# Attention feeding a two-layer network on one core: another planner, another order for the first pairs, a later load of the output weights

## The chip, the cores and the metric

The kernel runs on one core of one Trainium2 chip. The metric is the device time of one execution in microseconds (us), as the median of eleven runs of the kernel before. The profile is of one further look at the same program: its span runs from the first to the last instruction on the core.

## The reference

There are 8 batches of 8 heads with 576 positions and head width 64. Each head is computed twice: once with queries, keys and values averaged over groups of 4 positions (144 positions), and once in a window of fewer than 4 positions to either side. The two are added, the heads are laid side by side, and the 4608 x 512 matrix `x` goes through two matrix products with the function h/(1+exp(-h)) between them.

```python
out_d = sm_attn(mean4(q), mean4(k), mean4(v))          # 144 positions
out_up = np.repeat(out_d, 4, axis=2)
mask = np.abs(pos[:, None] - pos[None, :]) < 4
out_local = softmax(where(mask, scale * q @ k.T, -1e9)) @ v
x = (out_up + out_local).transpose(0, 2, 1, 3).reshape(4608, 512)
h = x @ w_in                                           # 512 x 2048
g = h * (1.0 / (1.0 + np.exp(-h)))
return g @ w_out                                       # 2048 x 512
```

## The kernel before

**Pairs.** Two heads make a pair `p`, 32 in all; four pairs make a batch. The work of one pair on TensorE (PE) is cut into units, each a function of the builder: `T` (36 transposes of queries and keys, 72 instructions with their weight loads, line 572), `S` (scores: 20 local matmuls, then 8 with the averaged queries and keys), `Z` (the sums of both softmaxes), `VP` (averages of the values), `PV` (the products with the values) and `RB` (spreads the reciprocal sums over the rows). From pair 10 on, unit `V(n)` joins S of pair n, T of n+1, Z of n-1 and PV of n-2, and from pair 10 the reciprocals take a way through DRAM instead of RB.

**What stands around a unit.** A pair's `q` and `k` (two DMAs of 288 KB, into 4 buffers `qk`) and its `v` (four of 80 KB, into `vs`) come on SyncE's queue, SP. `c` casts q and k on GpSimd, POOL (line 544; on VectorE, DVE, for pairs 0 and 1); `cw` casts the values (line 554). `eq` and `ek` bring T's result back on ScalarE, ACT; `mk` averages the keys on DVE (line 586) and `mq` the queries (two POOL instructions, lines 597 and 599, for pairs 0 to 7; DVE line 590 after). S waits for all of these; its last 8 matmuls for mq. `x` and `xd` are the exponentials on ACT (lines 624 and 626), `k` the mask on DVE (line 628). After Z: the reciprocal `r`, then `rh`, `rx`, `rm`, `rl` (lines 707 to 714) split it into three parts for RB, `eb` copies RB's result (ACT, line 735), `m` multiplies (DVE, line 745) and `a` adds both attentions into `xT` (POOL, line 769). RB and S share the PSUM tensor AB. PV and Z of pairs 0, 2 and from 4 on use CD, those of pairs 1 and 3 use HP, which the first matrix product uses too.

**The network.** `g1_j_f` is one tile of the first product: 512 rows (j, 9 of them) by 128 columns (f, 16), four matmuls; ACT takes a tanh (`t`, line 783) and DVE multiplies (`s`, line 785). `g2` is a quarter of a tile of the second product, four matmuls; four quarters make 128 rows of the output. g1 of j=0 needs `a` of pairs 0 to 3; g1 of j=1 also that of pairs 4 to 7. The weights are loaded from POOL's queue in eight pieces, `w0` to `w3` for w_in and `w4` to `w7` for w_out.

**Order.** Nothing is ordered at run time: each engine runs a fixed list. The builder makes the units in a written order (lines 900 to 935). Then `Plan.order` (line 218) plays them through: each engine picks among the next few units (14 on PE, 30 on POOL, 40 elsewhere; on PE in the order made) one that is ready in its own accounting. Costs (`cost`, `dcost`), the latencies `LAT` and due times of the weights (`ready`, line 882) only decide the order; they are not waited for on the chip. A unit that is placed early on an engine holds up all that is listed behind it, as engines run in order.

Of the kernel before, what the change touches and what calls it, by code (L numbers as in the profile page):

```python
# [18 lines left out]
NVP = 14  # L19
NDIR = 10  # L20
NEQ = 12
NTH = 99
NMQ = 8


# [141 lines left out]
class Plan:  # L167


    LAT = {"PE": 0.25, "ACT": 0.2, "DVE": 0.2, "POOL": 0.2, "SP": 0.1}  # L170

    def __init__(self):
        self.units = []
# [13 lines left out]
    def op(self, u, fn, r=(), w=(), dma=None):  # L187
# [27 lines left out]
        pre.discard(u)  # L215
        u.pre |= pre

    def order(self, look, first):

        todo = {e: first.get(e, "").split() for e in Prog.ENGS}  # L220
        free = {e: 0.0 for e in Prog.ENGS}
        ring = {e: 0.0 for e in Prog.ENGS}
        for u in self.units:
            u.pre = {v for v in u.pre}
            u.npre = len(u.pre)
            for v in u.pre:
                v.succ.append(u)
        pend = {e: [u for u in self.units if u.eng == e] for e in Prog.ENGS}
        head = {e: 0 for e in Prog.ENGS}
        taken = set()  # L230
        res = []
        left = len(self.units)
        while left:
            best = None
            for e in Prog.ENGS:
                lst = pend[e]
                while head[e] < len(lst) and lst[head[e]] in taken:
                    head[e] += 1
                if todo[e]:
                    win = [next(u for u in lst[head[e]:] if u.name == todo[e][0] and u not in taken)]  # L240
                    if win[0].npre:
                        continue
                else:
                    win = [u for u in lst[head[e]:head[e] + look[e]] if u not in taken and not u.npre]
                if not win:
                    continue
                t = max(free[e], min(u.ready for u in win))
                c = min((u for u in win if u.ready <= t + 0.05), key=lambda u: (u.ready - 100000 if u.fifo else u.prio, u.idx))
                t = max(t, c.ready)
                if best is None or t < best[0]:  # L250
                    best = (t, c)
            t, u = best
            del todo[u.eng][:1]
            u.start = t
            free[u.eng] = t + u.cost
            if u.dcost:
                e = u.eng
                begin = max(t + u.cost + 0.4, ring[e])
                other = max(x for y, x in ring.items() if y != e)
                ring[e] = begin + u.dcost + min(u.dcost, max(0.0, other - begin))  # L260
                u.end = ring[e] + (3.2 if e == "ACT" else 1.6)
                if e == "SP":
                    free[e] = max(free[e], ring[e] - 4.0)
            else:
                u.end = t + u.cost + self.LAT[u.eng]
            for v in u.succ:
                v.npre -= 1
                same = v.eng == u.eng and not u.dcost
                v.ready = max(v.ready, t + u.cost + (0.06 if u.eng != "PE" else 0.0) if same else u.end)
            taken.add(u)  # L270
            res.append(u)
            left -= 1
        res.sort(key=lambda u: u.start)
        return res


def bass_hourglass_attn__then__act_silu_kernel(
# [9 lines left out]
    with kctx:  # L287
# [4 lines left out]
        def R(name, psum=False):  # L292
            if name not in res:
                res[name] = Res(name, psum)
            return res[name]
# [57 lines left out]
        def one(eng, name, cost, fn, r=(), w=(), dma=None, prio=None, dcost=0.0):  # L353
            u = L.unit(eng, name, cost, prio, dcost)
            L.op(u, fn, r, w, dma)
            return u
# [103 lines left out]

        def dma(eng, name, out_, in_, w, sem, dcost, r=(), prio=None, cost=0.42):
            return one(eng, name, cost, lambda s: s.dma_start(out_, in_), r, w, sem, prio, dcost)  # L464

        def tick(p, d):
# [53 lines left out]
        def load_w(c):  # L520
            if c < 4:
                return dma("POOL", f"w{c}", w_in_sb[:, :, 512 * c:512 * c + 512],
                           moe_w_in[:, 512 * c:512 * c + 512].rearrange("(kc p) f -> p kc f", p=128),
                           [R(f"w_in{c}")], f"w_in{c}", 3.1, cost=0.9)
            c -= 4
            return dma("POOL", f"w{c + 4}", w_out_bf[:, 4 * c:4 * c + 4, :],
                       moe_w_out[512 * c:512 * c + 512, :].rearrange("(f p) n -> p f n", p=128),
                       [R(f"w_out{c}")], f"w_out{c}", 3.1, cost=0.9)
# [199 lines left out]
        def RB(p):  # L728
            n = p % NR
            u = L.unit("PE", f"RB{p}", 0.45)  # L730
            for m in range(10):
                x, c = divmod(m, 5)
                mm(u, AB[:, x, 72 * c:72 * c + 72], sel[:, m, :], rpart[p % 2][:, 2, :],
                   selr + [rpr[p % 2][2]], [rAB[x]])
            one("ACT", f"eb{p}", 0.77, lambda e: e.activation(  # L735
                Rb[n][:, :].rearrange("p (x n) -> p x n", x=2), AB[:, :, 0:360], AF.Copy),
                r=rAB, w=[R(f"Rb{n}0"), R(f"Rb{n}1")])
# [69 lines left out]
        def T(p):  # L807
            made.add(("T", p))
            u = L.unit("PE", f"T{p}", 0.45 if p > 1 else 0.9)
            pe_T(u, p)  # L810
            after_T(p)

        def VP(p):
            u = L.unit("PE", f"VP{p}", 0.4 if p > 1 else 0.8)
            pe_VP(u, p)
            after_VP(p)

        def S(p):
            u = L.unit("PE", f"S{p}", 0.4 if p > 1 else 0.8)
            pe_S(u, p)  # L820
            after_S(p)

        def Z(p):
            made.add(("Z", p))
            u = L.unit("PE", f"Z{p}", 0.35 if p > 1 else 0.7)
            pe_main(u, None, p)
            after_Z(p)

        def PV(p):
            made.add(("PV", p))  # L830
            u = L.unit("PE", f"PV{p}", 0.45 if p > 1 else 0.9)
            pe_main(u, p, None)
            after_PV(p)
# [22 lines left out]
        def feed():  # L856

            for p in range(NPAIR):
                for name, fn, need in (
                    ("lqk", load_qk, ("c", NQK)), ("c", cast, ("T", NB - 1)),  # L860
                    ("lv", load_v, ("cw", NVS)), ("cw", castw, ("PV", NV)),
                    ("lvq", load_vq, ("cv", NVQ)), ("cv", castv, ("PV", NV)),
                ):
                    src = {"c": "lqk", "cw": "lv", "cv": "lvq"}.get(name)
                    if p < NVP and name in ("lvq", "cv"):
                        made.add((name, p))
                    if (name, p) in made or (src and (src, p) not in made):
                        continue
                    if p >= NTH and name[0] == "l" and ("x", p - (4 if name == "lqk" else 3)) not in made:
                        continue  # L870
                    if p >= need[1] and (need[0], p - need[1]) not in made:
                        continue
                    if name in ("lv", "lvq") and ("lqk", p) not in made:
                        continue
                    made.add((name, p))
                    fn(p)
# [2 lines left out]
        constants()  # L879
        feed()  # L880
        for c in range(8):
            load_w(c).ready = 16.0 + 5.0 * c
        todo = [(j, f) for j in range(NSUP) for f in range(16)]
        todo2 = [(j, tt) for j in range(NSUP) for tt in range(4)]

        def G1(n):
            for _ in range(n):
                if todo:
                    g1(*todo.pop(0))
# [7 lines left out]
            if parts[-1] == 3:  # L897
                todo2.pop(0)

        T(0)  # L900
        feed()
        for n in range(10):
            T(n + 1)
            feed()
            S(n)
            if n > 0:
                Z(n - 1)
            if n > 1:
                PV(n - 2)
                feed()  # L910
            if 0 < n <= NDIR:
                RB(n - 1)
            if 0 < n <= NVP:
                VP(n - 1)
            if n > 4:
                G1((2, 4, 4, 4, 2)[n - 5])
        L.boost = 0
        n = 10
        while todo or todo2:
            if n < NPAIR + 2:  # L920
                V(n)
                if n <= NDIR:
                    RB(n - 1)
                if n <= NVP:
                    VP(n - 1)
                feed()
            m = 4
            G1(1 if m else 0)
            G2((0,))
            G1(1 if m else 0)  # L930
            G2((1,))
            G1(1 if m else 0)
            G2((2, 3))
            G1(m - 3 if m else 0)
            n += 1
        P = Prog()
        for u in L.order({"PE": 14, "ACT": 40, "DVE": 40, "POOL": 30, "SP": 40}, FIRST):
# [36 lines left out]
```

## Time and profile before

| | |
|---|---|
| median of 11 runs | 359.32 us (357.58 to 361.86) |
| the profiled execution's own time | 359.32 us |
| its span, first to last instruction | 357.6 us |
| PE busy | 329.4 us (92%) |
| DVE, ACT, POOL busy | 222.0, 182.1, 156.3 us |
| bytes moved | 60.28 MB, mean 169 GB/s |
| first g1 matmul, first g2 matmul | 43.6 us, 77.9 us |
| V(10) begins on PE | 73.87 us |

1.7 us of the time lie outside the span. In the slices of the profile, each digit is the busy share of an engine in a fortieth of the span (8.9 us); in the table by stage, the busy time of an engine stands beside the number of its instructions in parentheses, then the clock granted to TensorE (1.00 is full), the share of the DMA engines and GB/s. In a list of instructions in order of time, the brackets at the end of a row hold the idle time before it and what ended it.

### The profile page before, as it was taken

The page shows a single profiled execution, that of the slowest core. Times are in us where ns is not written, and L with a number is a line of the kernel's source. Part 1 is how long each engine was busy: PE and PEld are TensorE (multiplying, and loading weights), DVE is VectorE, ACT ScalarE, POOL GpSimd, SP SyncE. Part 2 cuts the span into 40 slices and gives each one's busy share as a digit, 9 for nine tenths or more (in the row PEclk, how much of TensorE's full clock was granted, in tenths as well). Part 3 has the DMA queues.
Part 4 walks back from the last instruction along what each step waited for, and adds up shares of the span by engine and source line. Part 5 has one row for each costly group of instructions (what it writes and reads, how often), then busy time and mean ns, then how long its engine had stood idle before and what let it go on. Part 6 is the DMA issues. An engine that isn't in the chain of part 4 may idle for free.

```text
span 357.6 us, 10993 instructions
## 1 busy us (share of the span) xinstructions
PE 329.4 (92%) x4712; PEld 214.0 (60%) x4742; DVE 222.0 (62%) x392; ACT 182.1 (51%) x326; POOL 156.3 (44%) x203
## 2 busy tenths in 40 slices
PE   1674799989999999999999999999999999999996
PEld 0453677556666666666666666666665566666642
DVE  7585879986766677777767667666655434343400
ACT  2773668766555555455555555555553343434421
POOL 7948775651755566555565666553111100000000
PEclk9996589999999999999999999999999999999999
DMA  8999999997899978878777784132042000110012
GB/s 230 234 262 266 308 272 251 256 230 196 256 231 279 255 224 219 230 200 220 217 226 210 213 209 149 65 119 75 34 129 89 31 29 29 45 44 29 31 59 88
DMA packets 73506, 60.28 MB, mean 169 GB/s; under 512 B 47986, under 2 KB 55794, under 8 KB 73458
## 3 DMA queue, kind: packets, MB, share of 16 engines
q1 hardware_dynamic: 63818, 44.27, 45.4%
q10 hardware_dynamic: 5416, 9.02, 9.1%
q0 software_dynamic: 4224, 6.29, 7.9%
q8 instruction: 37, 0.61, 0.7%
q14 instruction: 11, 0.09, 0.1%
HBM read 51.76 MB, written 9.91 MB: 172 GB/s over the span
## 4 chain that ended last, share of the span: by engine, by line
PE 80%; DMA 6%; DVE 4%; SPq 3%; POOL 2%; issue 2%; ACT 2%; POOLq 0%; ACTq 0%
PE HP L359 36%; PE o L359 28%; PE pe_ L359 8%; PE CD L359 5%; DMA vs<-in_v_dram 4%; SPq L464 3%; PE AB L359 3%; DMA qk<-in_k_dram 3%; PE o L572 2%; DVE gT L785 1%; POOL qkb L544 1%; POOL vt L597 1%; DVE rrest L711 1%; DVE Pt L628 0%; DVE xo L745 0%
## 5 line engine op out<-in xcount | busy, mean ns | idle before, releaser
L359 PE MATMUL HP<-xT,w_in_sb 128*128 128x512 f32 x576 | 162.6, 419 | 0.3 <-DVE gT L785 0.2
L785 DVE SCALAR_TENSOR_TENSOR gT<-th,HP 128x512 bf16<-128x512 f32 x144 | 96.5, 683 | 100.7 <-ACT th L783 99.9
L783 ACT ACTIVATE th<-HP 128x512 f32<-128x512 f32 x144 | 86.1, 598 | 76.6 <-PE HP L359 73.9
L359 PEld LDWEIGHTS HP<-xT,w_in_sb 128*128 128x128 f32 x576 | 106.2, 190 | 27.4 <-DVE gT L785 0.7
L359 PE MATMUL o<-w_out_bf,gT 128*128 128x512 bf16 x437 | 101.8, 379 | 1.9 <-issue 0.2
L359 PEld LDWEIGHTS o<-w_out_bf,gT 128*128 128x128 bf16 x464 | 42.4, 98 | 55.1 <-issue 9.8
L769 POOL TENSOR_TENSOR xT<-xo 128x576 fp32r<-128x576 f32 (+3 forms) x48 | 44.2, 933 | 48.8 <-DVE xo L745 48.8
L800 ACT ACTIVATE osb<-o 128x512 f32<-128x512 f32 x29 | 17.3, 597 | 61.3 <-PE o L359 61.3
L554 POOL CAST vb<-vs 128x640 bf16<-128x640 f32 x30 | 21.7, 724 | 58.7 <-PE CD L359 43.1
L544 POOL CAST qkb<-qk 128x1152 bf16<-128x1152 f32 x30 | 34.4, 1146 | 5.3 <-DMA qk<-in_k_dram 5.0
L572 PE MATMUL o<-idn,qkb 64*64 64x64 bf16 x576 | 17.3, 203 | 15.2 <-POOL qkb L544 8.2
L745 DVE TENSOR_TENSOR xo<-CD,Rb 128x720 f32<-128x720 f32 x30 | 27.0, 899 | 1.3 <-ACT Rb L735 0.7
L559 POOL TENSOR_TENSOR vt<-vq 128x512 f32<-128x512 f32 x18 | 22.9, 1273 | 7.6 <-DMA vq<-in_v_dram 7.6
L359 PE MATMUL pe_<-w_out_bf,gT 128*128 128x512 bf16 x109 | 26.1, 380 | 0.2
L572 PEld LDWEIGHTS o<-idn,qkb 64*64 64x64 bf16 x576 | 13.7, 118 | 17.9 <-POOL qkb L544 8.9
L586 DVE TENSOR_REDUCE kd<-kT 128x144 bf16<-128x576 bf16 x32 | 23.4, 733 | 1.1 <-ACT kT L582 1.1
L582 ACT ACTIVATE kT<-pe_ 128x576 bf16<-128x576 bf16 x32 | 20.9, 652 | 1.8 <-PE pe_ L572 0.4
L624 ACT ACTIVATE Pt<-AB 128x576 bf16<-128x576 f32 x32 | 20.7, 648 | 1.2 <-PE AB L359 1.2
L572 PE MATMUL pe_<-idn,qkb 64*64 64x64 bf16 x576 | 16.5, 203 | 2.0 <-DVE qkb L541 1.0
L359 PEld LDWEIGHTS pe_<-w_out_bf,gT 128*128 128x128 bf16 x112 | 10.0, 98 | 13.6 <-issue 3.2
L590 DVE TENSOR_REDUCE qd<-qT 128x144 bf16<-128x576 bf16 x24 | 17.8, 743 | 0.0
L628 DVE TENSOR_TENSOR Pt<-Pt,mask_bf 128x576 bf16<-128x576 bf16 x32 | 16.3, 511 | 0.9 <-ACT Pt L624 0.9
(79 smaller groups left out, 314.1 us busy)
## 6 DMA issues: line engine op xcount, KB each, us to landing
vs<-in_v_dram SPq DMA_DIRECT2D x126, 80.0 KB, 4.2
qk<-in_q_dram SPq DMA_DIRECT2D x32, 288.0 KB, 4.7
out_dram<-osb SPq DMA_DIRECT2D x36, 256.0 KB, 3.3
qk<-in_k_dram SPq DMA_DIRECT2D x30, 288.0 KB, 5.6
Rb<-scr ACTq DMA_DIRECT2D x44, 180.0 KB, 4.6
vq<-in_v_dram SPq DMA_DIRECT2D x18, 256.0 KB, 5.6
w_in_sb<-in_moe_w_in_dram POOLq DMA_DIRECT2D x4, 1024.0 KB, 9.6
w_out_bf<-in_moe_w_out_dram POOLq DMA_DIRECT2D x4, 512.0 KB, 9.1
```

The lines of the kernel that those rows point to most:

```text
L359: L.op(u, lambda t: t.matmul(out_, lhsT, rhs, start=start, stop=stop, skip_group_check=True), r, w)
L544: one("POOL", f"c{p}", 1.15, lambda g: g.tensor_copy(qkb[j][:, :, :], qk[i][:, :, :]), r=[R(f"qk{i}0"), R(f"qk{i}1")], w=[R(f"qkb{j}0"), R ...
L554: one("POOL", f"cw{p}", 0.72, lambda g: g.tensor_copy(vb[m][:, :, :], vs[i][:, :, :]), r=rr, w=[R(f"vb{m}")])
L559: one("POOL", f"va{p}", 1.3, lambda g: g.tensor_tensor(vt[:, :, :], vq[i][:, :, 0:128], vq[i][:, :, 128:256], ALU.add), r=rr, w=[R("vt")])
L572: L.op(u, lambda e, o=o, w=w, j=j: e.transpose(o, w, idn[half(j), :]), [R("id"), R(f"qkb{n}{x}")], [rE if x else rF])
L582: one("ACT", f"ek{p}", 0.68, lambda e: e.activation(kT[j][:, 3:579].rearrange("p (g r) -> p g r", r=9), pe_[:, 0:288].bitcast(BF16).rearra ...
L586: one("DVE", f"mk{p}", 0.74, lambda e: e.tensor_reduce(kd[j][:, 0:SD], kT[j][:, 3:579].rearrange("p (g r) -> p g r", r=4), AX.X, ALU.add), ...
L624: one("ACT", f"x{p}", 0.66, lambda e: e.activation(Pt[m][:, :, :], AB[:, :, 0:288], AF.Exp, scale=0.125), r=rAB, w=[R(f"P{m}"), R(f"tick{p ...
L745: one("DVE", f"m{p}", 0.92, prio=-450000 if L.boost else None, r=rCD + [R(f"Rb{u}0"), R(f"Rb{u}1")], w=[R(f"xo{x}")], fn=lambda e: e.tenso ...
L769: one("POOL", f"a{p}", 0.15 + n * 0.0019, lambda g, dst=dst, in0=in0, in1=in1: g.tensor_tensor(dst, in0, in1, ALU.add), r=[R(f"xo{x}")], w ...
L783: one("ACT", f"t{j}_{f}", 0.62, lambda e: e.activation(th[tb][:, :], hps[hb], AF.Tanh, scale=0.5), r=[rH[hb]], w=[R(f"th{tb}")], prio=-1)
L785: one("DVE", f"s{j}_{f}", 0.71, lambda e: e.scalar_tensor_tensor(gT[j % 2][:, f, :], th[tb][:, :], 1.0, hps[hb], ALU.add, ALU.mult), r=[rH ...
```

## The change

`Plan.order` is written anew. It used to pick, event by event, with one running time for each DMA ring; it now steps a clock over all engines, lets the rings share one rate (`SHARE`, `WORK`), delays PE at each block of 256 instructions, slows PE's units before its time 52 and keeps certain DVE units and POOL's apart in time (`LOCK`). Its result is again only an order. The written order of the first ten pairs is new, as is the place of g1 and g2 among the later V units. Loads of pairs from 12 on wait for an exponential of a pair 3 or 4 before (`NTH` 99 becomes 12). The due times of w_in go from 16, 21, 26, 31 to 18, 23, 28, 33 and those of w_out from 36, 41, 46, 51 to 55, 60, 65, 70. `pace` is new but off (`CAP` is 0), `hold` stays empty and `WEIGHTS` is not used.

```diff
-NTH = 99
+NTH = 12
+CAP = 0
...
-            load_w(c).ready = 16.0 + 5.0 * c
+            load_w(c).ready = float((18, 23, 28, 33, 55, 60, 65, 70)[c])
...
-        T(0)
-        feed()
-        for n in range(10):
-            T(n + 1)
-            feed()
-            S(n)
-            if n > 0:
-                Z(n - 1)
-            if n > 1:
-                PV(n - 2)
-                feed()
-            if 0 < n <= NDIR:
-                RB(n - 1)
-            if 0 < n <= NVP:
-                VP(n - 1)
-            if n > 4:
-                G1((2, 4, 4, 4, 2)[n - 5])
+        hold = []
+        for x in """
+            T0 T1 S0 T2 S1 Z0 T3 S2 RB0 VP0 PV0 Z1 T4 S3 RB1 VP1 PV1 Z2 S4 RB2 VP2 PV2 Z3 RB3 VP3 PV3 T5
+            G2 S5 Z4 RB4 VP4 PV4 T6 G2 S6 Z5 RB5 VP5 PV5 T7 G3 S7 Z6 RB6 VP6 PV6 T8 G3 S8 Z7 RB7 VP7 PV7
+            T9 G4 S9 Z8 RB8 VP8 T10 G2
+        """.split():
...
-            m = 4
-            G1(1 if m else 0)
             G2((0,))
-            G1(1 if m else 0)
-            G2((1,))
-            G1(1 if m else 0)
-            G2((2, 3))
-            G1(m - 3 if m else 0)
+            G1(2)
+            G2((1, 2, 3))
+            G1(2)
```

In the list, `G2` stands for two tiles of g1, `G3` for three. What the planner makes of it, read from the built programs (the number after the letters is the pair):

```
PE before:   T0 T1 S0 T2 S1 Z0 VP0 T3 Z1 RB0 PV0 VP1 S2 T4 PV1 RB1 Z2 VP2 S3 T5 PV2 Z3 RB2 VP3 S4 T6 PV3 RB3
             Z4 VP4 S5 T7 Z5 RB4 g1_0_0 g1_0_1 PV4 S6 VP5 g1_0_2 RB5 g1_0_3 T8 S7 g1_0_4 Z6 g1_0_5 ...
PE after:    T0 T1 S0 T2 S1 Z0 T3 Z1 VP0 PV0 S2 T4 RB0 VP1 S3 PV1 Z2 RB1 VP2 S4 PV2 RB2 Z3 VP3 PV3 RB3 T5
             Z4 S5 VP4 g1_0_0 g1_0_1 RB4 PV4 T6 g1_0_2 g1_0_3 Z5 VP5 S6 g1_0_4 PV5 T7 RB5 g1_0_5 ...
POOL before: mq1 c3 mq2 cw2 w0 c4 mq3 cw3 c5 a0 w1 cw4 mq4 w2 a1 c6 cw5 mq5 a2 w3 c7 cw6 a3 w4 mq6 c8 cw7
             mq7 a4 w5 c9 cw8 w6 c10 cw9 a5 w7 c11 cw10 a6 ...
POOL after:  mq1 c3 cw2 w0 mq2 cw3 c4 w1 mq3 c5 mq4 a0 w2 cw4 a1 w3 c6 a2 cw5 mq5 a3 c7 cw6 cw7 c8 a4 mq6
             cw8 w4 cw9 mq7 a5 w5 c9 w6 a6 w7 cw10 a7 c10 ...
```

Up to V(10) the order before has 16 tiles of g1, the order after 19. From V(10) on both give each V four tiles of g1 and four quarters of g2.

## The prediction

> **What bounds the kernel now.** First the slices and busy times of the page.
>
> ```profile
> PE 329.4 (92%) x4712; PEld 214.0 (60%) x4742; DVE 222.0 (62%) x392; ACT 182.1 (51%) x326; POOL 156.3 (44%) x203
> ...
> PE   1674799989999999999999999999999999999996
> ...
> PEclk9996589999999999999999999999999999999999
> ```
>
> PE is full from the seventh slice on, and its work does not change. So the time is decided in the first 80 us: whatever PE leaves idle there is added at the end. The table by stage says where.
>
> ```profile
> 20.00:25.00 5.00, 4.66 (x162) 3.66 (x158) 3.76 (x8) 4.11 (x10) 1.70 (x3) 1.00 1.06 325
> 25.00:30.00 5.00, 0.82 (x60) 0.82 (x60) 1.73 (x6) 1.15 (x3) 2.02 (x2) 0.61 0.98 206
> ...
> 60.00:70.00 10.00, 9.48 (x203) 6.44 (x200) 10.00 (x16) 7.53 (x15) 6.67 (x7) 1.00 1.18 244
> 70.00:75.00 5.00, 3.76 (x114) 2.67 (x116) 3.60 (x8) 2.58 (x6) 2.00 (x3) 1.00 1.18 257
> ```
>
> In order PE, PEld, DVE, ACT, POOL, clock, DMA. At 25 to 30 PE stands still; from 60 to 70 DVE is full, and PE's 9.48 is not at its peak. The list of POOL's instructions in order of time names the transfers behind it:
>
> ```profile
> 18.78 1.16 POOL L544 CAST qkb<-qk 128x1152 bf16<-128x1152 f32 x1
> ...
> 22.28 0.72 POOL L554 CAST vb<-vs 128x640 bf16<-128x640 f32 x1 [1.21 <-DMA vs<-in_v_dram]
> 27.98 1.15 POOL L544 CAST qkb<-qk 128x1152 bf16<-128x1152 f32 x1 [4.99 <-DMA qk<-in_k_dram]
> ...
> 45.58 0.68 POOL L597 TENSOR_TENSOR vt<-qT 128x288 f32<-128x288 bf16 x1
> ...
> 49.57 0.72 POOL L554 CAST vb<-vs 128x640 bf16<-128x640 f32 x1 [1.72 <-DMA vs<-in_v_dram]
> ```
>
> By their order these are c4, cw3, c5, mq6 and cw7. The waits of PE (in total, times, longest) agree:
>
> ```profile
> PE o L572 <- POOL qkb L544: 8.2, 4, 4.2
> PE AB L359 <- ACT Rb L735: 1.0, 1, 1.0
> ```
>
> Its longest wait, 24.97 to 29.18, is T5 for c5, and c5 for the keys of pair 5.
>
> **What the Trainium skill says.** "DMA: Bandwidth & Descriptors", section Issuing engines are not separate DMA queues: loads from SP, ACT and POOL run on the same 16 engines and interleave. The trace agrees: pair 4's q and k, issued at 13.5, landed in 3.9 to 4.2 us; pair 5's, issued at 18.2 beside w0, took 7.5 to 9.0. "TensorE: Matmul & The Clock Gate", Part 1: the clock falls to half after an idle window of about 3.4 us and rises after as much work; here it is 0.61 at 25 to 30, and VP takes 0.93 us before the clock has risen, 0.56 after. "SBUF — State Buffer", on the shared port pair: certain VectorE and GpSimd operations exclude each other for a whole instruction; the trace has a 0.28 us `rx` of 2.69 us at 33.33, while POOL is busy without a break. "Runtime: NRT & Kernel Launch", Instruction fetch mechanics: instructions come in blocks of 256, mostly hidden; here PE's idle time put down to issue is 0.6 us in all, so replaying the blocks has little to win.
>
> **The change, part by part.** I follow the new lists with the durations of the old trace. A unit runs when its engine is free and its inputs are there.
>
> *1. c4 behind cw3.* On POOL, c4 ran at 18.78, before the values of pair 3 were needed. Now cw3 stands ahead, and those landed at about 22.3: cw3 to 23.0, c4 (1.15) to 24.1, so T4 at 24.2 instead of 21.39. RB0, formerly at 18.63, is listed behind T4: 24.9. PE idles some 3 us from about 21, where it was busy.
>
> *2. T5 behind PV3.* The 4.21 us wait for c5 leaves PE. Its cover is now the chain of pairs 0 to 3: RB0 24.9, S3 27.2 (AB is free after eb0), PV1 27.9, Z2 28.7 (CD is free after m0), RB1 29.3, VP2 30.1. S4's last matmuls need mq4, which stands behind c5: 28.0 to 29.1, mq4 to 30.2. S4 at 31.1 (eb1), PV2 31.8, RB2 33.1 (AB after x4, xd4: 0.65 and 0.53), Z3 33.9, VP3 34.5, PV3 36.0, RB3 37.4 (r 0.6, rh 0.26, rx, rm, rl some 0.8, with m2's 0.9 between), eb3 to 39.0, m3 to 40.0. T5 38.2, mq5 39.7 to 40.8, a3 to 42.0, S5 40.9, VP4 to 42.5: g1_0_0 at 42.6. Before: PV3 36.28, RB3 37.37, a3 43.62 to 44.82, so the two first tiles, begun at 43.62, ended at 47.0 (the fourth matmul needs a3). After: 42.6 and 3.4 us at half clock, 46.0. That is 1.0 us ahead, with T6, T7, Z5 and RB4 (0.4, 0.4, 0.35, 0.45: 1.6 us at full clock) not yet done. Net 0.6 us lost.
>
> *3. mq6 behind cw7, c8 and a4.* In the old list mq6 came before c8 (45.58) and S6 ran at 47.5. Now POOL does a3, c7, cw6 (to 43.9), then cw7 for the values of pair 7. These landed at 49.5. Do they come sooner? w1 is issued at about 24 instead of 30.24, but w0 landed only at 29.7 on the same queue; the gap in which that queue stood empty, 29.7 to about 30.9, is used, so w3 ends 1 to 2 us sooner than 49.2. Until then pair loads lag as much; after it they catch up. I take 49.4; bounds 47 (all of w_in out of the way early) and 51 (the lag not made up). cw7 to 50.1, c8 51.3, a4 (1.2) 52.5, mq6 (1.1) 53.6. PE comes to S6 thus: RB4 0.5, PV4 0.6, T6 0.4, two g1 at 0.93 (1.84 us for eight matmuls in the chain of waits), Z5 0.4, VP5 0.5: 4.3 us after 46.0, at 50.3. It waits 3.3 us; behind it in the list stand twelve tiles of g1, which need nothing from S6. By 53.6 the kernel before has also done T7, T8, S6, S7, RB5, Z6 and more than one g1: some 4 us of work.
>
> *4. From S6 to V(10).* Here DVE decided before (full from 60 to 70). In the new list from k6 (54.8) to s0_14: eleven s at 0.60, three m at 0.85, mk 0.7 x3, mq 0.7 x2, r 0.55 x3, k 0.4 x3, two triples rx, rm, rl at 0.77: 17.0 us, 0.4 until g1_0_4 has passed, and as much waiting for POOL's port as DVE had from 52 to 73, about 3 (k once 1.49, rl once 1.04, rx thrice over 0.6): 75.2. PE's own work to there is 19.2 from 53.6, so it is covered. g1_1_0 75.3, T10 0.4, RB8 0.45, two g1, V(10) at 78.9. It has three more tiles behind it than the old V(10) at 73.87: 78.9 less 2.8 is 76.1, 2.3 us late. Less of the 4 us than it seems, since in the old stretch PE needed 21.2 us for 17.1 of work; DVE made it slow, and now PE's lag hides there.
>
> *5. w_out later.* w4 follows cw8 on POOL at about 55 (before 44.78), w7 follows a6 at about 66 to 68 (63.18), landing 8.7 us later at 75 to 77. g2_0_0_3 comes at about 83: covered. If a6 slips, w7 slips with it; five us of slip would show. What the later w_out frees, transfers for pairs 8 to 10, held up no PE unit before (T8 50.7, c8 46.7): nothing won.
>
> *6. NTH, the pattern after V(10), pace.* SP now waits for x of pair p-4 before loading pair p; outputs queue behind. Two to three V periods of 8.65 us lie between load and use, against 4 to 10 us for landing: nothing. The same units per V: nothing, at most some tenths either way. pace is off.
>
> Sum: +2.3 us on the span of 357.6. The profiled execution's own time is 359.32, the same as the median, 1.7 above its span: 361.6.
>
> **The rivals.**
> - *DVE forgives more.* The triples and k now fall between POOL's operations: half of the 3 us of port waits go, PE limits at 53.6 + 19.2 = 72.8, V(10) at 76.8, net 74.0: 359.5. For it: nothing but order decides who blocks whom. Against it: POOL's own list is fuller there, with w4 to w7 and c9 moved in.
> - *Faster: the S6 wait does not bind.* mq6 ends 4.2 us after pair 7's values land, and PE comes to S6 at 50.3: it decides if they land by 46.1 (or PE comes 3.3 us later). Then S6 runs at 50.3 and DVE starts 3.3 us sooner: V(10) net at 72.8 to 71, by 1.1 to 3 below 73.87; 356.8 with PE's clock warm throughout. For it: after w3 nothing but pair loads is in flight. Against it: up to then w_in presses harder than before.
> - *Slower still.* The 3.3 us idle cools the clock (0.61 after the 4.2 us of before): up to 1.7 us more; a7, listed behind w7 and cw10, holds g1_1_0 by 1 us: 364.5.
> - *It doesn't do what it says:* g1 is not earlier by more than 1 us. That is part of my forecast, not another time.
>
> **How the numbers follow.** Forecast (361.6, own range 360.0 to 363.2) 0.55; DVE forgives (359.5) 0.14; faster (356.8) 0.20; slower still (364.5) 0.11. A difference below about 0.5%, 1.8 us, cannot be told from none. Of the forecast two thirds lie above 361.1: slower 0.37 + 0.11 = 0.48; same 0.18 + 0.14 = 0.32; faster 0.20. Range 356.5 to 365.0, which leaves out half of the faster case and little above.
>
> **What would show it.** Right: T4 at 23 to 25 with PE idle before it; no wait of T5 for c5; g1_0_0 at 41 to 44; S6 waiting for mq6 until 52 or later with cw7 behind a transfer; V(10) at 78 to 80. Wrong: cw7 before 46, or S6 without a wait; DVE with clear idle time at 60 to 70; g2_0_0 waiting for w_out.

## The result, and the profile after

The changed kernel takes **363.38 us** (median of 13 runs, 360.43 to 365.52), the kernel before 359.33 (50 runs). The ratio is 1.011, with a 95% interval from 1.0085 to 1.0134. So it is slower, by 1.1%. The forecast was 361.6, in a range of 356.5 to 365.0. All ratios in this text are of fast runs; only three runs, all of the experiment e10, were slow.

The profiled execution of the changed kernel has a time of its own of 365.1 us and a span of 363.4. As before, 1.7 us lie outside the span. It is 1.7 us above the median of its runs, so its waits are larger than a middling run has; a comparison with other profiles below says which.

First come the page's busy times and the slices that answer to those shown of before.

```profile
PE 329.5 (91%) x4712; PEld 214.8 (59%) x4742; DVE 227.2 (63%) x392; ACT 182.7 (50%) x326; POOL 158.1 (44%) x203
...
PE   0557757999999999999999999999999999999996
...
PEclk9998598999999999999999999999999999999999
```

PE does the same work: 329.5 us, against 329.4. From the eighth slice on it is as full as it was. The sixth and seventh slices, from 45.4 to 63.6 us, which held a 9 each before, hold a 5 and a 7 now. So the loss again lies in the first 80 us. The table by stage has, in this order, the stretch, its length, the busy time of PE, PEld, DVE, ACT and POOL with the number of instructions, the clock, the share of the DMA engines, and GB/s:

```profile
20.00:25.00 5.00, 2.38 (x99) 1.97 (x100) 2.82 (x7) 1.85 (x5) 3.41 (x6) 1.00 1.08 324
25.00:30.00 5.00, 4.34 (x101) 3.64 (x99) 2.95 (x6) 3.76 (x8) 4.62 (x7) 1.00 1.22 303
...
50.00:55.00 5.00, 1.76 (x36) 1.17 (x36) 3.07 (x5) 1.28 (x3) 4.40 (x6) 0.94 0.72 195
55.00:60.00 5.00, 5.00 (x102) 4.02 (x95) 2.85 (x4) 3.65 (x7) 0.00 (x0) 0.72 1.04 184
60.00:65.00 5.00, 2.45 (x99) 1.80 (x97) 2.14 (x3) 1.99 (x6) 4.07 (x6) 1.00 0.89 189
65.00:70.00 5.00, 4.65 (x69) 3.09 (x65) 4.93 (x9) 3.96 (x8) 1.88 (x3) 1.00 1.00 145
70.00:75.00 5.00, 5.00 (x99) 3.77 (x99) 4.93 (x12) 3.91 (x9) 2.21 (x3) 1.00 1.04 153
```

The stretch from 25 to 30, in which PE stood still before, is full now (4.34 of 5 us). In its place PE idles from 20 to 25 (2.38 us busy, before 4.66), and stands still twice later, from 50 to 55 and from 60 to 65. In between, the clock was 0.72 in the mean. The clock column is to be trusted only from the first change on record, here at 30.51 us: before it, it reads 1.00, but VP takes 0.93 us at 19.04, 0.94 at 29.29 (clock not yet risen) and 0.56 at 48.73, at full clock.

The waits of PE (in total, times, longest) name what it stood for:

```profile
PE AB L453 <- POOL qd L714: 8.1, 4, 3.7
...
PE CD L453 <- issue: 2.2, 2, 1.7
PE o L687 <- POOL qkb L659: 1.8, 2, 1.2
PE AB L453 <- DVE rp L829: 1.8, 3, 1.1
```

The waits for casts of keys, 8.2 us before, are down to 1.8. Waits of S for the averaged queries `qd`, which `mq` writes on POOL, have come in their place: 8.1 us, of which 1.6 belong to S0 at the start. The two longest are these rows of PE's list in order of time (start, length, instruction; in brackets the idle time before it):

```profile
49.23 0.35 PE L453 MATMUL AB<-qT,kT 64*64 64x58 bf16 x20
53.24 0.29 PE L453 MATMUL AB<-qd,kd 64*64 64x144 bf16 x8 [3.67 <-POOL qd L714]
...
59.95 0.35 PE L453 MATMUL AB<-qT,kT 64*64 64x58 bf16 x20
62.84 0.29 PE L453 MATMUL AB<-qd,kd 64*64 64x144 bf16 x7 [2.55 <-POOL qd L714]
```

These are S6 and S7: the 20 local matmuls run, and then the last 8 wait for mq6 and mq7. The two waits, 6.22 us, are all the idle time of PE from 45 to 65; in the kernel before it was 0.57 us there. POOL's list of the same time shows why mq6 and mq7 are late:

```profile
48.99 0.72 POOL L669 CAST vb<-vs 128x640 bf16<-128x640 f32 x1 [2.25 <-DMA vs<-in_v_dram]
49.66 1.15 POOL L659 CAST qkb<-qk 128x1152 bf16<-128x1152 f32 x1
50.76 1.20 POOL L884 TENSOR_TENSOR xT<-xo 128x576 fp32r<-128x576 f32 x1
51.93 0.66 POOL L712 TENSOR_TENSOR vt<-qT 128x288 f32<-128x288 bf16 x1
52.67 0.42 POOL L714 TENSOR_TENSOR qd<-vt 128x144 bf16<-128x144 f32 x1
53.04 0.72 POOL L669 CAST vb<-vs 128x640 bf16<-128x640 f32 x1
53.70 0.78 POOL L579 DMA_DIRECT2D w_out_bf<-in_moe_w_out_dram  x1
60.85 0.71 POOL L669 CAST vb<-vs 128x640 bf16<-128x640 f32 x1 [6.38 <-DMA vs<-in_v_dram]
61.53 0.66 POOL L712 TENSOR_TENSOR vt<-qT 128x288 f32<-128x288 bf16 x1
```

By their order these are cw7, c8, a4, mq6 (two rows), cw8, w4, cw9 and the first half of mq7. Twice POOL stands at a cast of values, cw7 and cw9, whose transfer has not landed. Each time a `mq` that PE needs sooner stands behind it. V(10) starts on PE at 83.59 instead of 73.87. It has three more tiles of g1 behind it, at 0.93 us each; so it is 6.9 us late, and the span is 5.8 us longer. In all nine profiles in which PE has the changed kernel's list (this one, e1 to e6, e9 and e12), the span ends 279.8 us after the start of V(10), within 0.1 us. So what these kernels differ in is decided before V(10).

### The profile page after: what moved, and what is told of

Read it like the earlier page. It is cut to its first block, busy times and chain, and to the rows that moved or that the text cites. A ratio compares the mean times of both kernels' runs of the same rounds, so it can differ in the third digit from the quotient of the medians.

```text
span 363.4 us, 11005 instructions
## 1 busy us (share of the span) xinstructions
PE 329.5 (91%) x4712; PEld 214.8 (59%) x4742; DVE 227.2 (63%) x392; ACT 182.7 (50%) x326; POOL 158.1 (44%) x203
## 4 chain that ended last, share of the span: by engine, by line
PE 79%; SPq 6%; POOL 4%; DMA 4%; DVE 3%; issue 2%; ACT 1%; POOLq 0%; ACTq 0%
PE HP L453 35%; PE o L453 27%; PE pe_ L453 7%; SPq L579 6%; PE CD L453 4%; PE AB L453 3%; POOL xo L476 2%; DMA vs<-in_v_dram 2%; DMA qk<-in_k_dram 2%; PE o L687 2%; DVE rrest L826 1%; DVE gT L900 1%; POOL vt L712 1%; DVE rp L828 0%; PE pe_ L687 0%
## 5 line engine op out<-in xcount | busy, mean ns | idle before, releaser
L453 PE MATMUL HP<-xT,w_in_sb 128*128 128x512 f32 x576 | 160.6, 418 | 0.4
L453 PEld LDWEIGHTS o<-w_out_bf,gT 128*128 128x128 bf16 x464 | 42.6, 98 | 54.9 <-issue 8.4
L884 POOL TENSOR_TENSOR xT<-xo 128x576 fp32r<-128x576 f32 (+3 forms) x48 | 45.1, 952 | 39.7 <-DVE xo L860 39.6
L743 DVE TENSOR_TENSOR Pt<-Pt,mask_bf 128x576 bf16<-128x576 bf16 x32 | 17.8, 557 | 3.7 <-ACT Pt L739 3.7
```

The source lines that it names most:

```text
L453: L.op(u, lambda t: t.matmul(out_, lhsT, rhs, start=start, stop=stop, skip_group_check=True), r, w)
L884: one("POOL", f"a{p}", 0.15 + n * 0.0019, lambda g, dst=dst, in0=in0, in1=in1: g.tensor_tensor(dst, in0, in1, ALU.add), r=[R(f"xo{x}")], w ...
```

## The experiments

All experiments were timed against the kernel before, which was run again beside each group of them (medians from 359.27 to 359.99). The ratios are estimates over the runs and not quite the quotients of the medians: for e3 these would give 360.43/359.80 = 1.0018, inside its interval. In the builder, the table `FIRST` can hold an engine's list of units, which is then taken instead of what the planner chooses. Except for e8 and e11, every kernel below holds all lists of one of the two kernels there, and only the units named in its diff stand elsewhere. So PE, ACT, DVE and SP keep their order. A ratio below 1 is faster than before.

| | edit | median us (runs) | ratio to before, 95% interval |
|---|---|---|---|
| after | | 363.38 (13) | 1.0110 [1.0085, 1.0134] |
| e1 | after, mq6 earlier | 362.16 (19) | 1.0053 [1.0031, 1.0075] |
| e2 | after, mq7 earlier | 362.45 (15) | 1.0066 [1.0042, 1.0091] |
| e3 | after, mq6 and mq7 earlier | 360.43 (14) | 0.9999 [0.9972, 1.0026] |
| e12 | after, w4 later | 362.41 (9) | 1.0085 [1.0049, 1.0121] |
| e6 | after, c4 earlier | 363.40 (6) | 1.0097 [1.0059, 1.0134] |
| e5 | e3, c4 earlier | 359.21 (14) | 0.9980 [0.9961, 1.0000] |
| e9 | e5, w1 to w3 later | 360.89 (22) | 1.0019 [1.0004, 1.0034] |
| e4 | after, no NTH | 363.47 (6) | 1.0089 [1.0056, 1.0122] |
| e7 | before, w_out later | 358.46 (22) | 0.9971 [0.9947, 0.9995] |
| e10 | e7, c6 and c7 earlier | 359.62 (22) | 0.9987 [0.9967, 1.0007] |
| e8 | the change without its planner | 368.10 (6) | 1.0228 [1.0198, 1.0258] |
| e11 | the new planner alone | 363.72 (6) | 1.0113 [1.0065, 1.0161] |

**The waits for mq6 and mq7: e1, e2, e3.** The theory: nearly all of the loss is S6's and S7's waits, made by POOL's order. The rival: they are only where a late head shows, and PE would wait elsewhere without them. e1 moves mq6, e2 mq7, e3 both.

```diff
 e1, POOL: ... c7 cw6
+mq6
 cw7 c8 a4
-mq6
 cw8 w4 cw9 mq7 a5 ...
```

> All five engine lists are those of the changed kernel; on POOL alone mq6 stands before cw7 instead of behind a4. Theory A (POOL's list holds S up, at S6 and again at S7): the 3.67 us wait of S6 goes, but mq7 still stands behind cw9, whose values landed at 60.85, so S7 waits some 5 to 6 us instead of 2.55; the time falls by 0 to 1.5 us, to 362 to 363.4. Rival B (what costs is the DMA share, not the list): S6 waits elsewhere for as long, no change. Rival C (one wait is all): 3.5 us less, about 360.

```diff
 e2, POOL: ... cw7 c8 a4 mq6 cw8
+mq7
 w4 cw9
-mq7
 a5 w5 ...
```

> Lists of the changed kernel; on POOL alone mq7 stands before w4 instead of behind cw9. Theory A: S6's 3.67 us stay, S7's 2.55 go; the time falls by 1.5 to 2.5 us, to 361 to 362. Rival B: no change. With DVE as the bound of that stretch the gain would be under 1 us.

e3 makes both moves.

> Both moves. Theory A: both waits go, 6.2 us of idle PE, of which DVE takes some back; the time falls by 3 to 6 us, to 357.5 to 360.5, at or below the kernel before. Rival B (DMA share): under 1 us. DVE-bound rival: 1 to 2 us.

Measured: against before, the changed kernel's 1.1% falls to 0.53% with mq6 moved, to 0.66% with mq7 moved, and to nothing with both (0.9999). The parts of 0.57 and 0.44 points make up 1.01 of the 1.11 of e3. The interval of e2 just touches that of the changed kernel; those of e1 and e3 lie clear of it. So moving two units of 1.1 us each in POOL's list, with all other lists as they were, takes away the loss. The moves do shift one more thing: w4, now listed behind mq7, goes out at 58.66 in e2 and 58.40 in e3 instead of 53.70. The waits of PE in e2:

```profile
PE AB L453 <- POOL qd L714: 4.9, 2, 3.6
```

S6 waits as before, 3.6 us; S7's wait is gone. In e1 S6 does not wait. Nor does S7, for which 5 to 6 us were expected, though mq7 stands behind w4 and cw9 there as in the changed kernel; so S7's wait is not a fixed part of that order (see e12). The profile also shows a second thing. The waits of PE in e1:

```profile
PE o L687 <- POOL qkb L659: 5.7, 2, 5.0
```

T4 waited for c4 for 5.0 us, against 1.23 in the changed kernel's profile. Its list up to there is the same. c4 stands behind cw3, and cw3 waits for the values of pair 3, whose landing varies from run to run: T4's wait was 0.4 us in e2's profile, 4.8 in e3's and 4.1 in e4's. So a single profile of these kernels is no measure of T4. What makes that landing vary was not tried.

**c4 ahead of cw3: e6 and e5.** This undoes step 1 of the prediction: alone in e6, on top of e3 in e5.

```diff
 e6 and e5, POOL: ... w0 mq2
-cw3 c4 w1 mq3
+c4 mq3 cw3 w1
 c5 mq4 ...
```

> The changed kernel with c4 and mq3 before cw3 and nothing else. Theory A: S6 still waits for mq6 behind cw7, whose values land when they land, so what T4 gains is waited away at S6: 0 to 1 us below 363.4. Rival (T4's delay is what the change costs): 2.5 us or more, to 361 or below.

> The lists of e3 (mq6 before cw7, mq7 before w4), and on POOL c4 and mq3 stand before cw3, as in the kernel before. Theory A (the head's lag was T4 behind cw3, 1.2 us of wait in the changed kernel's profile and 4.8 in e3's): T4 runs at 21 to 22, and without S6's wait the gain now arrives at the end: 1.5 to 3.5 us below e3's 360.4, so 357 to 359, below the kernel before. Rival (the chain of pairs 0 to 3 or the loads decide, not T4): within 0.7 us of e3.

Measured: e6 takes 363.40, as the changed kernel does. In its profile T4 no longer waits, and S6 waits until 54.58 instead of 53.24; its waits of PE:

```profile
PE AB L453 <- POOL qd L714: 8.1, 4, 5.2
```

What the head gains, S6 waits away: it waits 5.2 us instead of 3.7, since mq6 hangs on pair 7's values (cw7 at 50.33) and not on PE. The table by stage of e6 shows what the longer wait costs besides:

```profile
50.00:55.00 5.00, 0.42 (x9) 0.32 (x9) 1.06 (x3) 0.00 (x0) 4.59 (x6) 0.92 0.96 220
55.00:60.00 5.00, 5.00 (x81) 3.77 (x82) 1.26 (x3) 3.23 (x6) 2.34 (x5) 0.50 0.97 205
```

After 5.2 us of idle time PE runs at 0.50 for five microseconds. With the two `mq` moved too, e5 is at 0.9980, and e3 at 0.9999. The intervals overlap, so whether c4 is worth anything once the `mq` are early is not settled.

**Is it w4 that makes cw9 late? e12.** In the changed kernel w4 is issued at 53.70, while the values of pair 9 are in flight. In the kernel before it went out at 44.78.

```diff
 e12, POOL: ... mq6 cw8
-w4
 cw9 mq7
+w4
 a5 w5 ...
```

> The lists of the changed kernel on every engine; only POOL's differs: w4 (w_out's first piece, 512 rows of 2 KB) is issued after cw9 and mq7 instead of before them. In the changed kernel w4 was issued at 53.70, while the values of pair 9 were in flight, cw9 waited 6.38 us for these until 60.85, and S7 waited 2.55 us for mq7 behind cw9. Theory A (the second wait comes from step 5: w4 shares the DMA engines with pair 9's values): without w4 they land about 3 us sooner, cw9 at 57 to 58.5, mq7 before 60, S7 without a wait, and the time falls as it did when mq7 alone was moved, about 0.9 us, to 362.4 (0.2 to 0.4% below the changed kernel). Rival B (pair 9's loads are late by themselves, since they are issued late, and w4 does not matter): cw9 still at 60 to 61, S7 waits over 2 us, time unchanged at 363.4.

Measured: cw9 at 57.25 and S7 without a wait, as theory A said, and 362.41; the interval overlaps that of the changed kernel. But this alone decides nothing, since cw9 comes early in e4 and e6 too (56.65 and 57.63), where w4 stands ahead of it as in the changed kernel. In e4:

```profile
55.19 0.78 POOL L579 DMA_DIRECT2D w_out_bf<-in_moe_w_out_dram  x1
56.65 0.71 POOL L669 CAST vb<-vs 128x640 bf16<-128x640 f32 x1 [0.69 <-PE CD L453]
```

The single loads say more. These rows of the DMA view give the size of each and the median time from issue to landing: of the changed kernel, the three pieces of pair 9's values that were issued before w4, and the fourth, issued 0.08 us after it; of e6, pair 9's values, all issued before w4, and three pieces of pair 10's, issued after it; of e12, all values from 51 to 62 us, with w4 out of the way until 59.85.

```profile
vs<-in_v_dram SPq DMA_DIRECT2D x3, 80.0 KB, 3.2
vs<-in_v_dram SPq DMA_DIRECT2D x1, 80.0 KB, 6.8
...
vs<-in_v_dram SPq DMA_DIRECT2D x4, 80.0 KB, 3.5
vs<-in_v_dram SPq DMA_DIRECT2D x3, 80.0 KB, 8.3
...
vs<-in_v_dram SPq DMA_DIRECT2D x11, 80.0 KB, 3.3
```

So values issued right behind w4 land late, and theory A has the mechanism. But which values these are is decided by some tenths of a us. In the changed kernel's profile it was one piece of pair 9, for which cw9, mq7 and S7 had to wait. In e4 and e6 w4 went out at 55.19 and 55.04, after all of pair 9's values, and slowed only those of pair 10. How often S7 waits in the changed kernel, one profile cannot say.

**The loads' waits: e4.** Only `NTH` goes back to 99; the lists stay.

```diff
-NTH = 12
+NTH = 99
```

> Lists of the changed kernel, but loads of pairs from 12 on no longer wait for an exponential (NTH 99). Theory A: nothing, 363.4 within 0.5 us, as these loads come long before their use. Rival D (the waits on SP starve the loads around 60 to 75, where GB/s fell to 145 to 153): 1 us or more faster.

Measured: 363.47, no difference that can be told. In its profile T4 ran late (26.95), and S6 waited only 0.7 us: head and S6's wait trade against each other here too.

**w_out later, in the order before: e7 and e10.** The lists are those of the kernel before. e10 also moves two casts of keys.

```diff
 e7, POOL of before: ... cw6 a3
-w4
 mq6 c8 cw7 mq7 a4
-w5
 c9 cw8
-w6
+w4
 c10 cw9 a5
-w7
+w5
 c11
+w6
 cw10 a6
+w7
 ...
 e10, in addition: ... cw4 mq4
+c6
 w2 a1
-c6
 cw5 mq5 a2
+c7
 w3
-c7
 cw6 ...
```

> The kernel before with its lists, only w4 to w7 moved back on POOL, to behind cw8, a5, c11 and a6. Theory A (step 5 of the prediction): covered, nothing won or lost, 359.3 to 360 like the kernel before. Rival E (the later w_out itself costs, by pressing on loads at a worse time or by coming late): 1 us or more slower. Rival F (it helps): 1 us or more faster.

> e7 (the kernel before with w4 to w7 later) with c6 before w2 and a1, and c7 before w3 on POOL. In e7 PE waits 2.75 us for c6 and 2.65 for c7. If these waits reach the end: 1 to 2.5 us below e7's 358.5. If the chain of pairs 2 and 3 or the loads take over: the same within 0.7 us.

Measured: e7 at 0.9971, whose interval ends just below 1; e10 at 0.9987, which cannot be told from before or from e7. So the later w_out costs nothing in that order and is worth some 0.3%, if anything. There mq7 stands ahead of w4, at 51.52, and no `mq` behind a cast that w4 holds up. e7 is the best version found, below what was set as told from no change (0.5%).

**w_in later: e9.** In e5 PE has waits of 2.0 us that no semaphore ends. Its waits of PE:

```profile
PE CD L453 <- issue: 4.1, 2, 2.0
PE AB L453 <- DVE rp L829: 2.7, 3, 1.9
```

e9 moves the issues of w1 to w3 later on POOL.

```diff
 e9, POOL of e5: ... c4 mq3 cw3
-w1
 c5 mq4 a0
-w2
 cw4
+w1
 a1
-w3
 c6 a2 cw5 mq5 a3
+w2
 c7 cw6 mq6 cw7
+w3
 c8 ...
```

> e5's lists (mq6, mq7, c4 early), and on POOL w1 moved to behind cw4, w2 to behind a3, w3 to behind cw7, so that w_in no longer presses on the loads from 25 to 45. Theory G (w_in's haste delays pair loads and PE's own instruction blocks: e5's PE waits 4.1 us put down to issue at 38.3 and 48.6, the kernel before none there): issue waits under 1 us, cw6 and cw7 earlier, 1 to 3 us below e5's 359.2. Rival H (the issue waits come from the order of small matmuls, not from DMA): they stay at 3 to 4 us, time within 0.5 us. Rival I (w_in comes too late): g1_0_8 or g1_0_12 waits for it, slower.

Measured: 360.89, ratio 1.0019. This is no gain but a loss of some 0.4% on e5; the two intervals do not overlap. The waits of PE in e9:

```profile
PE AB L453 <- DVE rp L829: 4.1, 3, 2.3
...
PE CD L453 <- issue: 0.5, 1, 0.5
```

The waits put down to issue do go, from 4.1 us to 0.5, when nothing but the times of w_in's loads is changed. Waits of RB for the last term `rl` of the reciprocal's split, on DVE, come in their place. Which of the later loads costs the time was not tried.

**The planner and the written order apart: e8 and e11.** e8 is the whole change with the old `order`. e11 is the new `order` with the old written order, due times and NTH.

```diff
 e8, against after:
-    WORK = (("lkx", 1.4), ("lq", 1.05), ("lk", 1.05), ("lvq", 0.5), ("lv", 0.38), ("z", 0.4), ("b", 0.85))
-    LOCK = ("k", "cq", "ck", "rm", "rl", "rx")
-    def _model(self, u):
...
+    LAT = {"PE": 0.25, "ACT": 0.2, "DVE": 0.2, "POOL": 0.2, "SP": 0.1}
     def order(self, look, first):
+        ring = {e: 0.0 for e in Prog.ENGS}
...
 e11, against after:
-NTH = 12
+NTH = 99
-            load_w(c).ready = float((18, 23, 28, 33, 55, 60, 65, 70)[c])
+            load_w(c).ready = 16.0 + 5.0 * c
-        for x in """
+        for n in range(10):
+            T(n + 1)
...
```

> Everything of the change but the new order function: the old planner makes the lists out of the new written order, the new due times and NTH. On POOL it puts c4 before cw3, but mq6 and c7, c8 as it likes (mq6 before c8 and cw7, mq7 behind cw9 and w4). Theory A: where mq6 stands decides; no wait of S6 for cw7, but mq7 behind cw9 and S7 late: 360 to 362.5. Rival (the written order itself costs, whatever planner): 363 or more.

> Only the order function of the change, on the written order, due times and NTH of before. On POOL it puts c4 behind cw3, w1 and a0, and mq6, mq7 before w7 and cw7. With the old planner on the new written order at 368.1 and the whole change at 363.4, the new planner is worth 4.7 us there. If it is better by itself: 356 to 359. Theory A (c4 and the chain behind it are late, but S6 and S7 do not wait): 359.5 to 362.5.

Measured: the new planner on the old order costs 1.1%, the new order under the old planner 2.3%, both together 1.1%. So the costs do not add: each half is bad alone, and the new planner takes back half of what the new written order costs. The waits of PE in e8:

```profile
PE AB L359 <- DVE rp L714: 7.8, 3, 4.7
PE AB L359 <- POOL qd L599: 7.1, 2, 5.5
```

Here too the longest of these waits is one for a `mq` on POOL, 5.5 us, but at S4: mq4 stands behind cw4, whose values had not landed. S7, where the wait was expected, has none, and the time is far above the 360 to 362.5 expected. In e11's profile RB waits 2.9 us for a reciprocal on DVE at 41.19, and V(10) starts at 76.49, 2.6 us late at the same number of tiles. Which unit's place causes this was not tried.

## Why the prediction was right, and where not

The sign, the place and, up to S6, the mechanism were right. The time is 1.8 us above the forecast, inside the range. Two of its own signs went against it: V(10) came at 83.59 and not at 78 to 80, and DVE had clear idle time from 60 to 65 (busy 2.14 of 5 us).

- *Step 1, c4 behind cw3*: right. Foreseen 24.2 for T4, measured 24.01, with PE at 2.38 of 5 us from 20 to 25. What it missed is that this start varies by some 4 us between runs, and that, alone, it costs nothing that can be told (e6 at 363.40): S6's wait covers it.
- *Step 2, T5 behind PV3*: right. T5 runs at 37.84 without a wait for c5, and g1 starts at 42.11 (foreseen 42.6). Within the step there was one unforeseen wait: PV2 stopped for 1.67 us, put down to issue.
- *Step 3, mq6 behind cw7, c8 and a4*: right, nearly to the number. cw7 at 48.99 (values foreseen at 49.4), mq6 done at 53.1 (53.6), S6 reached at 49.23 (50.3), wait 3.67 us (3.3). e1 shows that it counts: 0.57 points of the 1.1. That the sizes agree so closely is in part luck: in e4, with the same lists, PE came late and S6 waited 0.7 us.
- *Step 4, from S6 to V(10)*: this step failed. It took DVE as the bound, with PE covered, and gave V(10) at 76.1 after allowance for the three tiles; it came at 80.8. DVE was busy for only 2.85 and 2.14 us in the two stretches from 55 to 65: PE, at half its clock and then waiting, gave it nothing to do. From 65 on DVE was full, as foreseen (4.93 of 5 us), only later. Two terms were left out. One is the clock after S6's wait: it was at half from 54.40 to 57.82, which by estimate costs half of these 3.4 us, 1.7. The prediction had this only in the rival "slower still", at just this size. The other is S7's wait for mq7, 2.55 us. The prediction followed POOL's list only as far as mq6 and did not ask who waits behind cw9. Together these are 4.3 of the 4.7 us in this profile. In a middling run the second need not occur: e4 and e6, as slow as the changed kernel, have no wait at S7, and their V(10) starts at 81.72 and 82.77. With mq7 moved (e2) the ratio of 1.0066 times 359.3 is 361.7 us, which is the forecast; its interval runs from 360.8 to 362.6.
- *Step 5, w_out later*: right for what waits on w_out. The first quarter of g2 ran at 86.16, right after its V(10), and PE never waited for w_out, though w7 was issued at 70.70, three to five microseconds later than foreseen. Wrong that only PE's use of w_out matters: w4, moved from 44.78 to 53.70, held up a piece of pair 9's values in the profile, and cw9, mq7 and S7 behind it; in other runs it meets pair 10's (e12). In the order before, the same move is harmless or better (e7).
- *Step 6, NTH, pattern, pace*: NTH right (e4). From V(10) to the end of the span the changed kernel needs 279.8 us and, with the three tiles added, 282.6, against 283.7 before: nothing lost there, at most a microsecond won. The pattern after V(10) was not tried by itself.

The rival that lost in mechanism was "the S6 wait does not bind": S6 waited in every profile in which mq6 stood behind cw7, least in e4 (0.7 us), where PE came late. "DVE forgives more" was wrong too; DVE was not what decided between 53 and 65. "Slower still" came nearest in size, with its clock and with another second wait than a7's. Two small sums of the rivals do not close and touch nothing else: 361.6 and its 1.7 and 1 us make 364.3, not 364.5; and "DVE forgives more" puts V(10) 4.0 us behind its 72.8, where the forecast has 3.7 behind 75.2.

The prediction leaned on the Trainium skill for the blocks of instructions ("Runtime: NRT & Kernel Launch", Instruction fetch mechanics, mostly hidden) and concluded from 0.6 us of issue waits in the kernel before that there was little to win. That holds for the kernel before. In the changed kernel these waits are 2.2 us on CD alone, in e5 4.1 us. They are blocks of instructions that arrive late, and the profiles show it. There are 19 stops of 0.4 us or more put down to issue, in twelve of the fourteen profiles. The numbers of PE instructions before them (961, 1217, 1473, 1985 and so on) differ by multiples of 256, to within one, and each stop ends 1.3 to 1.6 us after a 16 KB load of instructions has landed. That the loads of w_in make these blocks late rests on e9 alone.

The clock agrees with "TensorE: Matmul & The Clock Gate", Part 1, in that it is judged in free-running windows: in every trace its changes lie on one grid of 3.41 us. The traces differ from the page's one idle window, and from the prediction's reading of it, in how much idle time it takes. In e5 a wait of 2.02 us was enough to halve the clock for the next 3.4 us:

```profile
46.60:48.50 1.90, 0.00 (x0) 0.00 (x0) 0.51 (x1) 0.56 (x1) 0.47 (x2) 1.00 1.11 253
49.00:52.50 3.50, 3.50 (x59) 2.32 (x62) 3.22 (x4) 1.68 (x5) 2.97 (x3) 0.52 1.08 231
```

In the changed kernel S7's wait of 2.55 us was not, as it fell on two windows, 0.93 us in one and 1.61 in the other:

```profile
60.50:62.70 2.20, 0.00 (x0) 0.00 (x0) 0.71 (x2) 0.00 (x0) 1.77 (x4) 1.00 1.25 252
63.00:66.00 3.00, 3.00 (x80) 2.08 (x72) 1.95 (x2) 2.79 (x6) 3.00 (x4) 1.00 0.52 88
```

## What to carry to other kernels

Where engines run fixed lists, follow each unit that a scheduler has put behind a wait for a transfer, to the end of the list and not only to the first one that binds: here moving two 1.1 us units ahead of such casts was worth the whole 1.1%. A load moved to a time when its user has long to wait is not free: ask whose transfer is in flight then, and what stands behind that transfer's user. And a unit started sooner ahead of a wait that does not move gains nothing, and the longer idle time can slow the clock as well. In e5, 2.02 us of idle PE that fell in one window of the clock were followed by 3.4 us at half of it, by estimate another 1.7 us.

## What the runs showed of the hardware

Values of 80 KB issued just behind a load of 512 KB from another queue took 6.8 us (changed kernel) and 8.3 us (e6) from issue to landing; those issued just ahead of it took 3.2 and 3.5 us. This is not the only thing that delays them: in e1 pair 9's values took 5.7 to 6.2 us, and no piece of w_out had been issued yet.

In the changed kernel's profile the share of the DMA engines was 1.00 and 1.04 from 65 to 75 us at 145 and 153 GB/s, and 1.08 from 20 to 25 us at 324 GB/s. So a full share does not tell the rate; what makes the difference was not tried.

PE's waits put down to issue changed from 4.1 to 0.5 us between two kernels (e5, e9) that differ only in when three loads are issued. All 19 such stops in the profiles lie on one grid of 256 PE instructions.

In the first 100 us of the fourteen profiles the clock changed only on a grid of 3.41 us. Of the windows that began at full clock, all with 1.78 us or more of idle PE (eleven windows) ended at half, and none with 1.2 us or less did; between these, both occurred. The clock rose only at the end of windows with at most 0.35 us of idle PE. The first rise on record came at 22.69 us in the kernel before, at 30.51 in the changed kernel and at 51.69 in e1. Up to there PE ran at half its clock, and for how long differs much between the profiles.
